# Down projection of an RWKV-7 and MLP kernel: from one plain product to seven half-size products

## The chip, the core and the metric

The kernel runs on one core of a Trainium2 chip. A core has five engines that run side by side, each with its own list of instructions worked off in order: TensorE (PE in the profile, with its weight loads as PEld), VectorE (DVE), ScalarE (ACT), GpSimd (POOL) and SyncE (SP), which here only issues transfers (DMAs). TensorE reads its operands in SBUF and writes its results to PSUM; the others bring them from PSUM to SBUF. The metric is the device time of one execution in microseconds.

## The reference

The reference is an RWKV-7 recurrence whose output goes through a two-layer MLP. Cut to what matters:

```
state = zeros(4, 8, 40, 40)                     # batch, heads, 40 x 40
for t in range(768):
    y[:, :, t] = einsum('bhd,bhde->bhe', r_t, state)
    Sa    = einsum('bhde,bhe->bhd', state, a_t)
    state = state * w_t - einsum('bhd,bhe->bhde', Sa, b_t) + einsum('bhd,bhe->bhde', v_t, k_t)
x = y.transpose(0, 2, 1, 3).reshape(3072, 320)   # 4 * 768 tokens
h = x @ w_in                                     # 320 -> 2048
g = h / (1 + exp(-1.702 * h))
out = g @ w_out                                  # 2048 -> 320
```

The change is about the last line. All arithmetic is float32.

## The kernel before

The 768 steps are cut into 12 chunks of 64 steps. A chunk is worked as two units of two batches each (24 units, `i`; chunk `c`, half `p`). For a unit, the attention part solves the recurrence inside the chunk with small matrix products (PSUM tiles `ps_N`, `ps_level`, `ps_Q`, `ps_T`, `ps_B`, `ps_X`, `ps_y` and so on), each followed by a copy or an elementwise operation on ACT, DVE or POOL, and most of these feed the next product. The unit's output is written to DRAM and read back in another layout into `xT_all`, which has three slots, one for each chunk (`part_with`, `get_back`).

The MLP (`mlp(c)`) works on the 256 tokens of a chunk. `up` makes the hidden layer in four quarters `q` (`ps_up`); `gelu` (L1000) brings each quarter from PSUM into a tile `g` with 512 hidden channels: `g_of(n)` is [128, 2, 2, 256], that is half-quarter `m`, block `f`, 256 tokens, of which 128 belong to each unit `p`. Then `down(p)` makes the output for the 128 tokens of one unit: eight parts `m`, each 2 blocks x 4 array quarters of 64 x 64, with 320 columns moving, all into one PSUM pair (two banks, one for each row half). `finish` brings it out: a copy of one bank (L1027, ACT or DVE), an addition of the other (L1029, DVE), and two stores on SP. Only the very last unit is cut into two column halves of 160. A float32 product takes two passes, so each `mm` (L301) shows as two matmul records, each with its own weight load: 16 records for a part.

The heart of the order is a list written out by hand. `plan.add` collects 2709 tasks in the order in which the program text adds them, with their dependences. The string `ORDER` then lists them as they are issued: the task's number, the engine that takes it (`p` PE, `a` ACT, `d` DVE, `g` POOL, `s` SP), and the PSUM pair (0 to 3) or, for transfers, how many may be under way. The costs given to `plan.add` stand only for whoever made the list; at run time the list alone counts. Each engine works its tasks strictly in that order, so a task that waits holds up all that stands behind it on its engine.

SBUF is nearly full: `w_sb` holds both weight matrices, `extra` is scratch for the conversion of the weights at the start and free afterwards, and `plan.slots` says how many buffers each tile has.

Of the kernel before, what the change touches and what calls it, by code (L numbers as in the profile page):

```python
# [109 lines left out]
0s 8s 1s4 5s 102a 7s 6s 3a 9s 157a 87p0 88p1 10s 89a1 100p2 90a0 95d 13s4 4a 11s 93d 12s 101d2 98p3 2s 94d 97d 17s 103p1 16s 96d  # L110
142p0 15s 104a1 105d1 141p2 143a0 106d 99d3 107p1 144a2 18s4 148g 132p3 108a1 109d1 155p0 45s4 149d 27s 150g 156d0 158p2 14s4
110p1 159a2 160d2 91s4 130p0 161d 19a 24s4 112d1 162p2 111a1 22d 26s4 25s 163a2 113p1 20d 131a0 152g 164d2 34s4 92a 272s 21d
165p0 114a1 151g 271s 147a 153p2 115d1 273s 166a0 167d0 116p1 23g 28a 154d2 262p0 343s 117d1 263p2 133a3 342s 264a2 118d1 168p3
36s 31d 33s 119p1 276g 169a3 170d3 35s 120d1 42s 122a1 171p2 277d 278g 121a 43s 124d1 123a1 126p3 173d2 125a1 127d3 285a 29d
128p1 172a2 44s4 286p3 30d 54s4 37a 174p2 129d1 32g 51s4 288d3 134p1 178a2 146s4 175d2 145s 265a0 135d1 176a 187p0 289d 136p1
275s4 179a2 266g 61s 38d 138d1 188a0 341s 139s 287a3 181p0 39d 185p3 40d 137a1 177a2 290p1 313d 180a2 182a0 53s4 280g 279g 274s
186a3 183p2 292d1 281p0 291a1 333p3 41g 184d2 332p1 282d0 189p2 334a3 60s4 345s 314p0 190d2 316a0 346d 355a 191p3 347d 315d0
193d3 356p2 344s2 62s 140s 194s 195s4 192d3 293p0 335a1 358d2 46a 283p3 359d 317p1 294a0 295d0 349g 318a1 284d3 360p0 269a 348d
350g 296p1 336d 361a0 362d0 319p3 383d 357a2 297a1 298d1 384p0 321p2 49d 320a3 299p1 385a0 47d 322a2 63s4 363p3 300a1 301d1
323d2 386a0 302p1 364a3 365d3 353p0 351p2 306a1 48d 267s3 207p3 52s3 307a1 305d1 208p3 50g 268s3 64a 303d1 209p3 352d2 210p3  # L120
211p3 354d0 308a1 196p2 304a 212p3 65d 197p2 213p3 72s3 214p3 70s3 270d 55a 309p1 337s3 198p2 69s4 366p0 310a1 66d 199p2 367a0
200p2 58d 468p1 201p2 368d0 469a 473s 202p2 476s 203p2 67d 387p0 477s 470a1 490d 204p2 68g 480s 339a 205p2 369p1 388d0 206a2
215p3 371d1 218p0 219p0 56d 472s4 216p3 483g 71s4 220p0 217a3 471d 81s4 221p0 482d 79s 311p2 222p0 370a1 223p0 224p0 312d2 225p0
340d 372p3 229p1 478s4 376a3 230p1 57d 378a3 324p2 560s4 377a3 59g 226p0 78s4 375a3 325d2 231p1 73a 232p1 227p0 373d3 326p2 374d
228a0 389p3 484g 479s3 327d2 338s4 240p0 529d 390a3 481g 328d2 379p3 233p1 380a3 329d 234p1 391p2 485g 241p0 556s4 392d2 80s4
242p0 393d2 74d 486p3 235p1 487d3 530p2 236p1 75d 531a2 381p3 237p1 532a2 330s4 382d3 238p1 76d 491p2 394p3 494a2 493d2 77g
239a1 243p0 395d3 82a 488p1 557s3 396p3 489d1 474a 558s4 83d 331s 251p1 492d2 495d 252p1 84d 85d 253p1 398d3 86g 559s4 548p2
244p0 703s 397d3 549a 570d 553s 245p0 496d 550a2 552s 399d 497a 254p1 551g 554a 498p3 564d 400s 568p2 565g 499a3 246p0 569d2
500d3 563g 247p0 562d 694p2 561g 255p1 248a0 401s2 249d0 475d 256p1 250s 533p3 257p1 534a3 555d 695a 571p0 535p3 573d0 258p1
574a0 698s4 501d 696a2 609d 502g 536a3 537p2 572d0 259a1 576d 566p3 538a2 702s 402p0 575g 567d3 577a 403p0 404p0 539d2 785s3  # L130
700a 405p0 706s 708d 406p0 578p3 407p0 580d3 408p0 260d1 610p2 409p0 581d 709g 410p0 611d2 411p0 612d2 503p1 707d 582g 412a0
424p2 425p2 504d1 704s2 426p2 505d1 427p2 697d 428p2 579d3 613p1 701d 429p2 614a1 583p0 430p2 584a0 506d 431p2 585d0 432p2 507a
782s2 586d 433p2 587d 446p3 434a2 508p1 588p0 509a1 447p3 590d0 589a0 510d1 261s2 413p2 511d 699s 414p2 591d 512a 783s 415p2
592g 416p2 513p0 417p2 514a0 515d0 593p1 516d 418p2 594a1 595d1 419p2 596d 420p2 517a 597d 421p2 422p2 518p0 423a2 435p1 519d0
436p1 521d0 520g 437p1 522d0 438p1 523d0 439p1 440p1 524d0 525p2 716p0 526a2 441p1 717d0 927s 442p1 718d0 527p2 443p1 719d0
444p1 528d2 598p0 721d 445a1 540p2 720d 722g 601d0 603a0 617p1 602d0 541d2 448p3 618a1 604d0 542p2 619d1 599d0 600d 615p1 705s
544d2 449p3 616a1 781s 710d 545g 711d 605p0 723p1 606a0 450p3 607p0 451p3 546s 608d0 930s 452p3 725d1 724d1 620p0 726d 543d2
727a 773p1 453p3 621d0 778s 774a 547s 754d 728p2 622p0 454d3 455d3 729d2 456s 457p3 775a1 776g 730d2 784s 786g 779a 777s 624d0
458p3 623d0 625g 731d 793p1 833d 732a 459p3 733p2 789g 460p3 626s 734a2 794d1 735d2 714p0 790g 736d 461p3 780d 737g 1009s 918p1
755p2 923s 462p3 715d0 756a2 627s 757a2 788d 463p3 738p0 787d 464p3 739a0 740d0 919a 795p2 465d3 758p0 1006s 466d3 798a2 921d  # L140
650p3 467s 759d0 920a1 651p3 924a 928s 796d2 712p1 797d2 652p3 922s 800d 799g 653p3 932d 801a 654p3 834p0 655p3 713d1 656p3
657p3 835d0 760p2 836d0 925d 658p3 761a2 659p3 762p1 660a3 741d 628p0 742d 926s 629p0 630p0 763d1 802p2 764d1 631p0 803a2 804d2
632p0 805d 633p0 806a 743p3 634p0 746d3 635p0 747d3 837p1 931g 748d3 636p0 838a1 1007s 749d3 637p0 807p2 744d3 933g 638a0 639p1
808d2 640p1 791p3 745a 809d2 672p0 810d 792d3 811a 750p2 641p1 751a2 812p3 642p1 813a3 814d3 752p2 643p1 753d2 644p1 815d 645p1
816a 765p3 839p2 766d3 646p1 840a2 647p1 817p3 648p1 818a3 819d3 767p2 820d 649a1 821d 673p0 769d2 929s 768d2 770g 822p3 934d
674p0 825a3 826a3 940p1 827a3 675p0 1151s 828a3 935d 943a1 771s 661p2 823d3 662p2 941d1 1154s 824a 663p2 942d1 997p3 945d 944g
664p2 998a 1002s 978d 938p1 946g 665p2 939d1 666p2 772s 667p2 668p2 829p1 669p2 999a3 1000d 1001s 830d1 670p2 1003a 1011d 676p0
671a2 1004d 831p3 841p1 677p0 832d3 1005s 842d1 936p3 843d1 678p0 937d3 844p2 679p0 845d2 947p1 1010g 680d0 846p3 948a1 681d0
1012d 682s 683p2 847d3 1013g 1008s 848d3 1019p0 1014g 949d1 684p2 1022a0 1230s 849d 1233s 979p3 685p2 980a3 950d 850s 1020d0
981a3 951g 1142p1 1021d0 686p2 1024d 1143a 1147s 1023d 1025g 982p3 1057d 687p2 1152s 952p0 851s 983a3 1145g 688p2 1156d 1146s  # L150
953a0 954d0 984p3 1144a1 955d 1148a 689p2 956d 985a3 1149d 986p0 690p2 987a0 1150s 988d0 957p1 691a2 863p3 958a1 692d2 864p3
959d1 865p3 693s 960d 866p3 961d 1026p0 867p3 1027a0 1028d0 868p3 1029d 1155g 869p3 1157d 1030a 1058p2 870p3 871p3 1059a2 872p3
1060d2 1031p1 873a3 852p0 1033d1 853p0 1034d 854p0 1035d 1061p2 855p0 1062d2 1032a1 856p0 962p3 857p0 963a3 964d3 1036p1 965d
858p0 1037a1 1038d1 859p0 1039d 1015p2 966a 1040g 860p0 1016d2 861p0 967p3 862a0 874p1 968d3 875p1 970d3 969g 1041p2 971d3 876p1
1042a2 972d3 877p1 973d3 878p1 879p1 1043d2 1017p0 1044d 974p3 1045a 880p1 1018d0 1231s 881p1 975a3 1164p2 882p1 1167a2 1165d2
1375s 976p0 883p1 1166d2 896p3 1169d 1168g 884a1 977d0 885p2 1170a 1046p0 989p1 1049a0 886p2 1050a0 990d1 887p2 1051a0 888p2
1052a0 889p2 1047d0 991p1 1048a 1065p0 992d1 1158g 1153s 890p2 1159d 1066a0 891p2 892p2 1067d0 1378s 893p2 1202d 1063p0 993d1
894p2 994d 1064a0 1229s 1053p1 897p3 895a2 1054d1 995s 1171p0 1221p2 898p3 1172a0 1173d0 1226s 1174d 1222a 1175g 1055p1 899p3
1056d1 1068p0 996s 1162p1 1223a2 1224d 1234g 1225s 1069d0 900p3 1227a 1163d1 1160p2 901p3 1236d 1161d2 902p3 1235d 1176p0 1228d
903p3 1177a0 1178d0 1243p1 904a3 1179d 1070p2 1246a1 1454s 905d3 1180g 1244d1 906s 1245d1 907p0 1248d 1232s 1237g 1071d2 1249a  # L160
908p0 1238g 1072d2 1247d 1181p3 1457s 1281d 1366p1 909p0 1182a3 1073d 1371s 910p0 1183d3 1367a 1074s 1184d 1250p2 1185d 911p0
1368a1 1369g 1370s 1380d 1251a2 1186p3 1252d2 1372a 912p0 1253d 1188d3 1254g 1075s 1187a3 1189d 1241p1 1373d 913p0 1190g 1255p2
# [87 lines left out]
def rwkv7_gelu_quick(ctx: ExitStack, tc: tile.TileContext, time_d, v_d, w_d, wc_d, ak_d, b_d, rv_d, w_in, w_out, out):  # L250
# [13 lines left out]
    EARLY = 4  # L264
    BY_PE = 4
    PLAIN = 4
    PARTS = 4
    ROUNDS, WINDOW, SHARE = 4, 5000.0, 1.0
    RANKS = [14, 16, 20, 24, 35, 37, 39, 41]
    HALF = [slice(0, 64), slice(64, 128)]  # L270
# [716 lines left out]
    def mlp(c):  # L987
# [16 lines left out]
        def down(p):  # L1004
# [28 lines left out]
            for n, cols in enumerate([slice(0, DM // 2), slice(DM // 2, DM)] if last else [slice(0, DM)]):  # L1033
                for m in range(NM):
                    part(m, n, cols)
# [7 lines left out]
        for p in BITS:  # L1043
            down(p)
# [105 lines left out]
```

## Time and profile before

| what | before |
|---|---|
| runs | 677.32, 679.32 and 683.4 us (median 679.32) |
| profiled execution, first to last instruction | 677.7 us |
| PE busy, weight loads busy | 649.6 us (96%), 568.7 us (84%) |
| DVE, ACT, POOL busy | 449.7 us (66%), 329.1 us (49%), 175.7 us (26%) |
| down product (`ps_down`), matmul records | 3200 |
| up product (`ps_up`), matmul records | 3840 |
| bytes moved | 69.74 MB |

The execution in the profile has a span of 677.7 us; no other time is given for it, and it lies 0.4 us above the lowest of the three runs and 1.6 us below their median. Each row of a group of instructions reads: line, engine, operation, out<-in, partitions x elements, count | busy time, mean duration in ns | idle time of the engine just before them, and what ended it. Matmul records overlap each other, because a matmul's own duration includes its way through the array; the spacing of many records in a row, as the chain of waits gives it (start, length, how many), says more than a mean.

### The profile page before, as it was taken

To read this page: it belongs to the slowest core of one execution; us is meant where nothing else is said; L and a number is where in the kernel's file an instruction comes from. 1 tells how busy PE (TensorE), PEld (TensorE's weight loads), DVE (VectorE), ACT (ScalarE), POOL (GpSimd) and SP (SyncE) were. 2 spreads that over 40 slices of the span, in tenths; PEclk is the share of its full clock that TensorE was granted. 3 is DMA by queue.
4 is the path that set the end of the run, shared out by engine and by line. 5 is a ranking of instruction groups with operands and counts; after the bars stand their busy time and mean duration, and the time that the engine had idled before them with its cause. 6 is when DMAs were issued, how large, how long until landed. Compare 5 with 4: busy or idle time off the path is not lost.

```text
span 677.7 us, 42447 instructions
## 1 busy us (share of the span) xinstructions
PE 649.6 (96%) x19616; PEld 568.7 (84%) x19616; DVE 449.7 (66%) x916; ACT 329.1 (49%) x681; POOL 175.7 (26%) x201
## 2 busy tenths in 40 slices
PE   5777999999999999999999999999999999999997
PEld 4667787787999997888888899999889798799896
DVE  5777779777867668757776687868656766675001
ACT  3676745634564655654545445455344454263010
POOL 6541443324123123123113211322411421300000
PEclk9979999999999999999999999999999999999999
DMA  6875753415324314432404513513412411200200
GB/s 208 295 255 160 226 172 97 129 42 152 107 64 131 94 58 124 114 107 65 124 14 131 149 35 108 155 33 107 140 38 62 130 53 45 69 15 14 60 13 21
DMA packets 35473, 69.74 MB, mean 103 GB/s; under 512 B 5472, under 2 KB 14816, under 8 KB 35296
## 3 DMA queue, kind: packets, MB, share of 16 engines
q1 hardware_dynamic: 35216, 66.99, 32.9%
q8 instruction: 154, 2.52, 1.6%
q14 instruction: 23, 0.19, 0.1%
q10 hardware_dynamic: 80, 0.04, 0.0%
HBM read 59.15 MB, written 7.86 MB: 99 GB/s over the span
## 4 chain that ended last, share of the span: by engine, by line
PE 88%; DMA 6%; DVE 2%; issue 1%; SPq 1%; ACT 1%; DVEq 0%; ACTq 0%
PE ps_up L301 31%; PE ps_down L301 29%; PE ps_level L301 8%; PE ps_y L301 5%; PE ps_B L301 4%; PE ps_X L301 2%; PE ps_N L301 2%; PE ps_rz L301 1%; PE ps_RV L301 1%; PE ps_A L301 1%; PE ps_zT L301 1%; SPq L331 1%; DMA w_sb<-in_w_in 1%; PE ps_cum L301 1%; PE ps_T L301 1%
## 5 line engine op out<-in xcount | busy, mean ns | idle before, releaser
L301 PE MATMUL ps_up<-xT_all,w_sb 64*64 64x256 f32 x3840 | 253.3, 377 | 2.1 <-issue 1.3
L301 PE MATMUL ps_down<-w_sb,g 64*64 64x320 f32 (+1 forms) x3200 | 241.5, 419 | 0.2 <-ACT zr L879 0.2
L301 PEld LDWEIGHTS ps_up<-xT_all,w_sb 64*64 64x64 f32 x3840 | 170.8, 133 | 18.8 <-issue 2.1
L301 PEld LDWEIGHTS ps_down<-w_sb,g 64*64 64x64 f32 x3200 | 142.5, 133 | 31.6 <-issue 0.4
L1000 ACT ACTIVATE g<-ps_up 128x1024 f32<-128x1024 f32 x48 | 49.2, 1025 | 46.3 <-PE ps_up L301 45.8
L719 POOL TENSOR_TENSOR EX<-ES,quads 128x512 f32<-128x512 f32 x30 | 39.7, 1324 | 116.4 <-DVE ES L712 77.7
L761 ACT COPY W<-ps_level 128x512 f32<-128x512 f32 x56 | 32.8, 585 | 67.7 <-PE ps_level L301 66.0
L301 PEld LDWEIGHTS ps_level<-W,EX 64*64 64x64 f32 x2560 | 60.0, 134 | 5.4 <-DVE T L840 0.2
L763 DVE TENSOR_TENSOR E<-two,ps_level 128x256 f32<-128x256 f32 x80 | 33.1, 415 | 36.5 <-ACT W L761 32.3
L301 PE MATMUL ps_level<-W,EX 64*64 64x64 f32 (+1 forms) x2560 | 56.8, 217 | 0.0
L717 ACT ACTIVATE EX<-ES,quads 128x256 f32<-128x256 f32 x82 | 37.2, 501 | 31.9 <-DVE ES L712 31.3
L629 POOL TENSOR_TENSOR ak<-ak,FT 128x512 f32<-128x512 f32 x17 | 23.0, 1353 | 77.2 <-DMA ak<-in_ak 54.4
L301 PEld LDWEIGHTS ps_level<-PT,EX 64*64 64x64 f32 x1280 | 30.7, 138 | 11.5 <-DVE EX L733 3.3
L301 PE MATMUL ps_level<-PT,EX 64*64 64x64 f32 (+2 forms) x1280 | 32.5, 234 | 6.9 <-DVE EX L733 5.0
L712 DVE STREAM_TRANSPOSE ES<-E 128x256 f32<-128x256 f32 x80 | 35.3, 443 | 4.4
L301 PE MATMUL ps_y<-RV,kh 64*64 64x104 f32 (+1 forms) x768 | 35.4, 247 | 0.9 <-DVE M L917 0.9
L301 PE MATMUL ps_y<-M,bh 64*64 64x104 f32 (+1 forms) x768 | 35.5, 247 | 0.7 <-DVE M L917 0.5
L901 ACT COPY B<-ps_B 128x416 f32<-128x416 f32 (+1 forms) x35 | 17.2, 493 | 34.4 <-PE ps_B L301 34.2
L301 PEld LDWEIGHTS ps_y<-RV,kh 64*64 64x64 f32 x768 | 29.6, 133 | 3.2 <-DVE M L917 1.5
L917 DVE TENSOR_TENSOR M<-ps_X,later 128x832 f32<-128x832 f32 (+1 forms) x24 | 23.9, 995 | 10.2 <-PE ps_X L301 10.0
L301 PE MATMUL ps_B<-RV,A 64*64 64x104 f32 (+1 forms) x768 | 29.2, 252 | 0.8 <-issue 0.8
L637 POOL TENSOR_TENSOR kh<-time,G 128x320 f32<-128x320 f32 x18 | 16.2, 901 | 51.2 <-PE ps_y L301 34.6
(133 smaller groups left out, 1099.0 us busy)
## 6 DMA issues: line engine op xcount, KB each, us to landing
ak<-in_ak SPq DMA_DIRECT2D x48, 160.0 KB
rv<-in_rv SPq DMA_DIRECT2D x48, 160.0 KB
time<-in_time SPq DMA_DIRECT2D x24, 320.0 KB
xT_all<-x_dram SPq DMA_DIRECT2D x48, 160.0 KB
wc<-in_wc SPq DMA_DIRECT2D x20, 264.0 KB
logw<-in_w SPq DMA_DIRECT2D x24, 160.0 KB
RV<-in_v SPq DMA_DIRECT2D x24, 160.0 KB
b<-in_b SPq DMA_DIRECT2D x48, 80.0 KB
```

The costliest lines, as they stand in the source:

```text
L301: nc.tensor.matmul(o, lhsT, rhs, start=start, stop=True, skip_group_check=True)
L331: begun.append(queue.dma_start(dst, src).ins)
L629: plan.add(R, {"DVE": 690.0, "POOL": 1270.0, "sbuf": True}, lambda t: of(t.engine).tensor_mul(ahT(), ahT(), FT_of(i)), reads=T("ak", "FT") ...
L637: plan.add(R + 4, {"POOL": 870.0, "DVE": 490.0, "sbuf": True}, lambda t, n=n, dst=dst: of(t.engine).tensor_mul(dst(i)[:, :, :D], by_head(t ...
L712: plan.add(rank, dve(256), lambda t: nc.vector.transpose(ES(n), source(t)), writes=[key("ES", n, 6)], **reads)
L717: nc.scalar.activation(dst[:, :, h], ES(n), ACT.Copy, scale=quads[:, h, :1])
L719: of(t.engine).tensor_mul(dst, ES(n).unsqueeze(2).to_broadcast([128, 8, 2, 32]), quads.unsqueeze(1).to_broadcast([128, 8, 2, 32]))
L761: plan.add(rank, any2(512), lambda t: copy(t.engine)(tiles_of(W(n + 1)), blocks(psum(t, ""), 64)), writes=[key("W", n + 1, 5)], pair=pair)
L763: plan.add(rank, dve(256), lambda t: nc.vector.tensor_sub(tiles_of(E(n + 1)), every(two32, [128, 2, 4, 32]), blocks(psum(t, ""), 64)[:, :, ...
L901: plan.add(R, any2(4 * wide), lambda t: copy(t.engine)(dst(), some(psum(t, "")[:, :, :208])), writes=[("Bv", i)] if x and c > 0 else T("B" ...
L917: plan.add(R + 1, dve(8 * wide), lambda t: nc.vector.tensor_tensor(M_of(i)[:, :, :wide].rearrange("p (j b) n -> p b j n", b=2), some(psum( ...
L1000: plan.add(-45, {"ACT": 1030.0, "table": "gelu"}, lambda t: nc.scalar.activation(g_of(c * NQ + q).rearrange("p m r n -> p r m n"), psum(t, ...
```

## The change

For chunks 1 to 11 (`FAST = 1`; chunk 0 keeps the plain product, now `plain`) the down product of a chunk is seen as a product of 2 x 2 blocks: A (256 tokens x 2048 channels) in token halves `p` and channel halves `m`, and B (`w_out`) in channel halves `m` and column halves of 160 (`HD`). Instead of eight block products, seven are made, by Strassen's scheme in Winograd's form:

- Sums of blocks of A, 128 x 256 elements for each quarter `q`: S1 = A22 - A21, S3 = A21 - A11 (in place of A21), S2 = S1 + A11, and S4 = A12 - S2 (in place of A12, once product 2 has read it). They are 16 tensor_tensor instructions a chunk, each on DVE or POOL as `ORDER` says: 67 of the 176 on DVE and 109 on POOL.
- Sums of blocks of B, made once (`weight_sums`): four instructions of 128 x 1280, three on DVE and one on POOL, into `extra`.
- Seven products (`times`), each of four parts of 16 matmul records, 64 x 64 weights and 160 columns. Products 1, 2 and 4 collect in the PSUM pair `fa`, 6, 5 and 7 in `fb`, 3 in `fc`.
- Bringing them out: for `fa` and `fb` a copy and a DVE addition of 480 columns each; five additions in SBUF on DVE or POOL (`cd`, `E`, `F`, `Q` and the output of token half 1); two DVE additions of 160 columns from `fc`; then two store tasks.

Places: S1 takes the third slot of `xT_all`, which leaves two for x; S2 overwrites the B12 block of `w_out` in SBUF, which is not read after the sums of B and chunk 0's product; the results of all products of a chunk lie in one buffer `sb` with a single slot, in place of `ob`. To make room, `wz` is now kept in place in `wch`, and two constants share a tile. The last unit is no longer cut in two.

`ORDER` has 3087 tasks. Up to the first part of chunk 0's down product the two lists name the same tasks on the same engines; behind it the order is new, and many other tasks have another engine: of the 24 x 4 block copies into `Tc`, DVE has 35 tasks instead of 52; of the outputs `x` (L962), 21 instead of 13; of the `W` copies (L761), 34 instead of 24; of the `zT` copies, 10 instead of 20; of the `P` copies (L702), 11 instead of 2.

```
-                     ... x=1, xT=3, g=4, ob=1), 4)
+                     ... x=1, xT=2, g=4, sb=1, S1=4, S2=4), 4)
...
-    wz_of = lambda i: buf("wz", i, [128, 8])
+    wz_of = lambda i: wch_of(i)[:, 0]
...
+    block = lambda n, p, m: g_of(n)[:, m, :, p * 128:p * 128 + 128]
+    S1_of = lambda n: xT_all[:, 2, (n % NQ) * 256:(n % NQ) * 256 + 256].rearrange("p (f t) -> p f t", f=2)
+    w_blocks = w_out_sb.rearrange("p (q m f n) -> p q m f n", q=NQ, m=2, f=2)
+    B = lambda m, n: w_blocks[:, :, m, :, n * HD:(n + 1) * HD]
+    S2_of = lambda n: w_blocks[:, n % NQ, 0, :, HD:HD + 128]
+    sums = extra.rearrange("p (k q f n) -> p k q f n", k=4, q=NQ, f=2)
+    def weight_sums():
+        made = [(0, B(0, 0), B(0, 1), ALU.subtract, []), (1, B(1, 1), sums[:, 0], ALU.subtract, [("sum", 0)]),
+                (2, B(1, 1), B(0, 1), ALU.add, []), (3, B(1, 0), sums[:, 1], ALU.subtract, [("sum", 1)])]
...
+        def fast():
...
+                combined(q, "S1", S1_of, a22, a21, ALU.subtract, [("weight", raws.index("x"))], [("S1", n)])
+                combined(q, "S3", a21, a21, a11, ALU.subtract, [("S1", n)], [("S3", n)])
+                combined(q, "S2", S2_of, S1_of, a11, ALU.add, [("S1", n), ("sum", 0), ("sum", 2)] + none, [("S2", n)])
+            def times(name, q, group, slot, left, right, reads, writes=[], first=False):
...
+                    for f in BITS:
+                        for r, b in QUARTERS:
+                            mm(ps[HALF[b], r, slot * HD:(slot + 1) * HD], a[HALF[r], f, b * 64:b * 64 + 64], right[HALF[r], q, f],
+                               fresh and f == 0)
...
+                times("1", q, "fa", 0, lambda n: block(n, 0, 0), B(0, 0), lambda n: [("g", n), ("weight", NQ + q)])
+                times("2", q, "fa", 1, lambda n: block(n, 0, 1), B(1, 0), ... , lambda n: [("P2", n)])
+                times("4", q, "fa", 2, lambda n: block(n, 1, 1), sums[:, 3], lambda n: [("g", n), ("sum", 3)])
+                combined(q, "S4", a12, a12, S2_of, ALU.subtract, [("S2", n), ("P2", n)], [("S4", n)])
+            evicted("fa", 0, 0)
+            add(lambda: sb_of(c)[:, 4::2], twice(0), sb(1, 2), wide, [("fa", c)], [("cd", c)])
+                times("6", q, "fb", 0, S2_of, sums[:, 1], lambda n: [("S2", n), ("sum", 1)])
+                times("5", q, "fb", 1, S1_of, sums[:, 0], lambda n: [("S1", n), ("sum", 0)])
+                times("7", q, "fb", 2, lambda n: block(n, 1, 0), sums[:, 2], lambda n: [("S3", n), ("sum", 2)])
+            evicted("fb", 1, 0)
+            add(sb(7), sb(0), sb(2), two, [("fb", c), ("fa", c)], [("E", c)])
+            add(sb(5), sb(7), sb(1), two, [("E", c), ("fb", c)], [("F", c)])
+            add(sb(3), sb(3), sb(1), two, [("fb", c)], [("Q", c)])
+            add(sb(6, 2), sb(6, 2), twice(3), wide, ... , [("out", 2 * c + 1), ("sb", c)])
+                times("3", q, "fc", 0, lambda n: block(n, 0, 1), B(1, 1), lambda n: [("S4", n), ("weight", NQ + q)])
+            for r in BITS:
+                plan.add(-45, dve(HD), lambda t, r=r: nc.vector.tensor_add(sb(5)(), sb(5)(), psum(t, "")[:, r, :HD].unsqueeze(1)), ...
```

The end of the new list, from the last hidden quarters of chunk 11 on, has on PE the parts of product 1, then 2 and 4 with those of 6 put between them, then 5, 7 and 3; on DVE, behind the addition of `fb`, stand `E`, `Q`, `F`, the output of token half 1, and then the two additions from `fc`.

More of the change, by code (lines that the diff above doesn't have):

```diff
@@ L114 @@
[L114 to L117, printed above, removed]
@@ L1013, in go @@
                             o = p * 128 + b * 64
-                            mm(po[HALF[b], r, :cols.stop - cols.start], g[HALF[r], f % 2, o:o + 64],
-                               w_out_sb[HALF[r], f * DM + cols.start:f * DM + cols.stop], f == 0)
+                            mm(po[HALF[b], r, :DM], g[HALF[r], f % 2, o:o + 64], w_out_sb[HALF[r], f * DM:(f + 1) * DM], f == 0)
                 parts = range(2 * m * DM // PIECE, (2 * (m + 1) * DM - 1) // PIECE + 1)
-                plan.add(R + 10 * (p + 1) + m + 8 * n, pe((2, cols.stop - cols.start)), go, reads=[("g", c * NQ + m // 2)] + [("weight", NQ + n) for n in parts],
-                         pair=("down", serial + n), most=1)
@@ L1020, in finish @@
-            def finish(n, cols):
-                ob, wide = lambda: ob_of(serial)[:, cols], cols.stop - cols.start
-                def store(t):
-                    for b in BITS:
-                        o = (2 * p + b) * S + c * C
-                        transfer(t, out[o:o + C, cols], ob()[HALF[b]], nc.scalar if last and n and b else nc.sync)
-                plan.add(-45, any2(wide), lambda t: copy(t.engine)(ob(), psum(t, "")[:, 0, :wide]),
-                         writes=[("ob", serial + n)], pair=("down", serial + n))
-                plan.add(-45, dve(wide), lambda t: nc.vector.tensor_add(ob(), ob(), psum(t, "")[:, 1, :wide]),
-                         reads=[("ob", serial + n)], writes=[("out", serial + n)], pair=("down", serial + n))
-                plan.add(-100, {"SP": 700.0}, store, reads=[("ob", serial + n), ("out", serial + n)], size=128 * wide * 4)
@@ L1033, in down @@
-            for n, cols in enumerate([slice(0, DM // 2), slice(DM // 2, DM)] if last else [slice(0, DM)]):
-                for m in range(NM):
-                    part(m, n, cols)
-                finish(n, cols)
+                plan.add(R + 10 * (p + 1) + m, pe((2, DM)), go, reads=[("g", c * NQ + m // 2)] + [("weight", NQ + n) for n in parts],
+                         pair=("down", serial), most=1)
+            for m in range(NM):
+                part(m)
+            ob = lambda: sb_of(c)[:, 4 + 2 * p:6 + 2 * p].rearrange("p h n -> p (h n)")
@@ new lines, in plain @@
+            plan.add(-45, any2(DM), lambda t: copy(t.engine)(ob(), psum(t, "")[:, 0, :DM]),
+                     writes=[("ob", serial)], room=[("sb", c)], pair=("down", serial))
+            plan.add(-45, dve(DM), lambda t: nc.vector.tensor_add(ob(), ob(), psum(t, "")[:, 1, :DM]),
+                     reads=[("ob", serial)], writes=[("out", serial), ("sb", c)], pair=("down", serial))
+            plan.add(-100, {"SP": 700.0}, lambda t: store(t, c, p), reads=[("out", serial)], uses=[("sb", c)], size=128 * DM * 4)
@@ L1042, in mlp @@
             gelu(q)
-        for p in BITS:
-            down(p)
+        if c < FAST:
+            for p in BITS:
+                plain(p)
+        else:
+            fast()
     for i in range(3):
@@ L1052, in rwkv7_gelu_quick @@
     weights()
+    weight_sums()
     for i in range(NU):
```

370 lines of the change are left out of this document (225 added, 145 removed).

## The prediction

> **What bounds the kernel now.** I read the page first, then the busy time by stage, then what PE waits for. From the page:
>
> ```profile
> span 677.7 us, 42447 instructions
> PE 649.6 (96%) x19616; PEld 568.7 (84%) x19616; DVE 449.7 (66%) x916; ACT 329.1 (49%) x681; POOL 175.7 (26%) x201
> ...
> PEclk9979999999999999999999999999999999999999
> ...
> PE 88%; DMA 6%; DVE 2%; issue 1%; SPq 1%; ACT 1%; DVEq 0%; ACTq 0%
> ```
>
> PE is busy 96% of the span, at the full granted clock but for the start, and holds 88% of the chain that ended last. A busy PE need not be the bound, so the stages, with busy time and instructions of each engine:
>
> ```profile
> core 0: us, PE busy (x) PEld busy (x) DVE busy (x) ACT busy (x) POOL busy (x), PEclk, DMA share, GB/s
> 0.00:100.00 100.00, 77.99 (x2598) 66.48 (x2600) 72.76 (x123) 59.64 (x141) 44.52 (x62) 0.97 0.69 219
> 100.00:600.00 500.00, 497.82 (x15286) 435.71 (x15279) 355.82 (x738) 252.33 (x515) 131.21 (x140) 1.00 0.32 92
> 600.00:678.00 78.00, 73.80 (x1755) 66.55 (x1746) 21.11 (x57) 17.10 (x27) 0.00 (x0) 0.99 0.09 24
> ```
>
> In the 500 us from 100 on PE lacks 2.2 us; in the first 100 it lacks 22. So behind the opening the kernel is a stream of matmuls, and what shortens it shortens the kernel, as long as nothing makes PE wait. The first 100 us hardly change: the two lists part at chunk 0's first down part, which this profile has at about 88 us.
>
> **What the stream gains.** The forms of the down product, and two stretches of the chain (start, length, records) in which it runs alone:
>
> ```profile
> L301 PE MATMUL ps_down<-w_sb,g 64*64 64x320 f32 x2944 | 232.8, 430 | 0.2 <-ACT zr L879 0.2
> L301 PEld LDWEIGHTS ps_down<-w_sb,g 64*64 64x64 f32 x3200 | 142.5, 133 | 31.6 <-issue 0.4 <-ACT zr L879 0.4
> L301 PE MATMUL ps_down<-w_sb,g 64*64 64x160 f32 x256 | 8.9, 296 | 0.0
> ```
>
> ```profile
> 626.30 10.77 PE ps_down L301 x159
> 659.72 14.10 PE ps_down L301 x336
> ```
>
> The stretch at 626 is ten parts of 320 columns (160 records, one missing): 10.77 / 10 = 1.077 us a part. The one at 659 is five such parts (80 records) and the 256 records of 160 columns: 14.10 - 5 x 1.077 = 8.71 us, or 34.0 ns a record and 0.544 us for a part of 16. That is the very form of the new products (64 x 64 weights, 160 columns), and it costs half of 1.077 and 6 ns more: halving the columns and doubling the weight loads is nearly free. A chunk has 16 wide parts now, 16 x 1.077 = 17.23 us, and will have 7 x 4 = 28 narrow ones, 28 x 0.544 = 15.24. That is 1.99 us less in ten chunks; the last, now 8 x 1.077 + 8.71 = 17.33, gives 2.09. Together **-22.0 us**. Chunk 0 keeps its product.
>
> Here a rule of the skill speaks against the change. The records of 133 ns for a weight load beside a set of four narrow matmuls in 4 x 34.0 = 136 ns leave little cover. The Trainium skill ("TensorE: Matmul & The Clock Gate", section "Back-to-back issue gap") says that pairs of weight load and matmul are spaced by both, 81 ns at 128 columns where the matmul alone takes 56: 25 ns more. Charged to each of 112 sets in 11 chunks this estimate is +31 us, and the term would be +9 instead of -22. The 256 narrow records measured here show no such 25 ns.
>
> **What the other engines get.** Rows for the new work (instructions of like size; in the second group the columns are count, then min/median/max in ns):
>
> ```profile
> L1027 ACT COPY ob<-ps_down 128x320 f32<-128x320 f32 x15 | 6.4, 426 | 29.6 <-PE ps_down L301 28.5 <-DMA xT_all<-x_dram 0.6 <-DMA rv<-in_rv 0.5
> L879 ACT COPY zr<-ps_rz 128x512 f32<-128x512 f32 x12 | 7.0, 586 | 21.0 <-PE ps_rz L301 20.9
> L1029 DVE TENSOR_TENSOR ob<-ob,ps_down 128x320 f32<-128x320 f32 x23 | 11.1, 482 | 19.8 <-ACT ob L1027 19.5
> L660 DVE TENSOR_TENSOR RV<-ps_RV,upper 128x512 f32<-128x512 f32 x24 | 16.2, 679 | 8.5 <-PE ps_RV L301 8.4
> L1029 DVE TENSOR_TENSOR ob<-ob,ps_down 128x160 f32<-128x160 f32 x2 | 0.6, 321 | 3.7 <-ACT ob L1027 3.7
> ```
>
> ```profile
> L707 DVE TENSOR_TENSOR PT<-two,PT x10: 381/416/1220, 102.9 to 536.2; 128x256 f32<-128x256 f32 x10
> L707 POOL TENSOR_TENSOR PT<-two,PT x10: 725/730/734, 119.9 to 591.3; 128x256 f32<-128x256 f32 x10
> L855 DVE TENSOR_TENSOR zr<-zraw,wz x22: 443/482/1562, 46.0 to 583.7; 128x320 f32<-128x320 f32 x22
> L962 DVE TENSOR_TENSOR x<-zr,FT x52: 275/280/1365, 89.8 to 627.7; 128x128 f32<-128x128 f32 x52
> L719 POOL TENSOR_TENSOR EX<-ES,quads x30: 1272/1280/1685, 118.6 to 597.7; 128x512 f32<-128x512 f32 x30
> ```
>
> DVE: 67 sums of 128 x 256 at 0.416 (L707) are 27.9 us. 22 additions of 480 columns from PSUM lie between 0.482 and 0.679, I take 0.64: 14.1. Four copies of that size on DVE, 2.6. 24 of the small additions at 0.31 to 0.48 (L962 to L855), 9. 22 additions of 160 columns at 0.321, 7.1. Three sums of weights, 1280 wide: by the step from 256 (0.416) to 512 columns some 1.5 us each, 4.5; the fourth, on POOL, some 3. PE needs the sums only from product 4 of chunk 1 on, and by the list 12 us of its other work lie between. Gone are 23 wide and two narrow `ob` additions but two, and all but one of DVE's `ob` copies, -14.5. The tasks that changed engine cancel to about +2 on DVE (fewer `Tc`, `zT` and spread tasks, more `W`, `x` and `P` ones). That is +53 us. POOL: 109 sums at 0.730 are 80 us, 31 small additions some 19, less 8 of moved work: +94 with the weight sum, to about 270. ACT gains about 9 and stays near half. All this is beside PE, and costs nothing while it is in time.
>
> What it does to DVE is the open price. Some 49 of the 53 us fall in the middle, which shrinks from 500 to about 479: 355.8 + 49 = 405 us, 85% instead of 71%. And the rows show DVE held up by POOL: with two inputs from SBUF the median of L855 is 482 ns, but the longest took 1562, 1.08 us more, most of a POOL instruction of L719. The mean excess of such DVE instructions is 0.08 us in L962 (mean 362, below), 0.15 in L707 (568), while the same operation with an input from PSUM has none (276):
>
> ```profile
> L962 DVE TENSOR_TENSOR x<-zr,FT 128x128 f32<-128x128 f32 x52 | 15.8, 362 | 0.2
> L962 DVE TENSOR_TENSOR x<-ps_y,FT 128x128 f32<-128x128 f32 x8 | 1.7, 276 | 0.5 <-PE ps_y L301 0.5
> L707 DVE TENSOR_TENSOR PT<-two,PT 128x256 f32<-128x256 f32 x10 | 5.7, 568 | 0.0
> ```
>
> POOL's share in the middle goes from 26% to about 46%, and some 340 DVE instructions with two SBUF inputs stand where some 230 did. At 0.07 us on the average now and, with POOL's share, 0.125 then, that is some 25 us more, and DVE is near 90%. Its list is worked in order, so work that comes late reaches PE. What PE waits for now, longest first:
>
> ```profile
> PE ps_level L301 <- DVE EX L733: 5.0, 6, 1.0
> ...
> PE ps_up L301 <- DMA xT_all<-x_dram: 0.6, 1, 0.6
> PE ps_zT L301 <- DVE zr L855: 0.6, 1, 0.6
> ```
>
> L733 belongs to the first four units, whose levels have a form of their own. For the middle I let the 2.2 us grow as DVE's free share shrinks, from 29 to 10%: 6.4, so **+4**. No row shows this directly. From below it is -2 (the new order removes today's waits), from above +12: each of the 11 chunks then loses about 1.1 us, one POOL sum of 0.73 and half of another, on some tight edge. I take the value near the lower end, since the list leaves the sums room: in most chunks the parts of 1, 2 and 4 (12 x 0.544 = 6.5 us) stand between the last `gelu` and product 6, and the chain `gelu`, S1, S2 is 1.02 (L1000 on the page) + 2 x 0.73 = 2.5. S4 has products 6, 5 and 7 for cover, another 6.5 us. Without that cover a chunk would pay up to 2.5 us.
>
> **Moved steps, queues and waits.** With two slots for x, the return of chunk c waits for `up` of chunk c-2, done a whole chunk before (some 45 us); free. The way through DRAM is 4.06 + 3.94 us and PE waits 0.6 for it in the whole run; uncovered it would cost 8 once. The single `sb` lets the copy out of `fa` wait for the stores of the chunk before; some 30 us of PE work lie between the last product of one chunk and the end of `fa` in the next, and a store lands in about 3. SP issues 24 stores instead of 25. PE gets 2 x 1984 more instructions (5184 down records instead of 3200), 10% of its list; its waits for issue are 1% of the chain, so 0 to 1 us, inside the +4.
>
> **The end.** There nothing hides the last steps. Now:
>
> ```profile
> 673.84 0.32 DVE L1027 COPY ob<-ps_down 128x160 f32<-128x160 f32 x1 [3.70 <-PE ps_down L301]
> 674.20 0.32 DVE L1029 TENSOR_TENSOR ob<-ob,ps_down 128x160 f32<-128x160 f32 x1
> 674.55 0.47 SPq L331 DMA_DIRECT2D out<-ob  x1
> 674.55 0.55 ACTq L331 DMA_DIRECT2D out<-ob  x1
> ```
>
> The last store is issued about 0.8 us after PE's end (673.8) and the span ends 3.15 later. Then: product 7 ends four parts, 2.18 us, before PE's end; behind it come the wait for PE (0.15), the ACT copy of 480 columns (0.426 to 0.586, say 0.55), the DVE addition 0.64, `E`, `Q`, `F` at 0.31, the output at 0.48 and the two additions of 0.321, with 0.04 between them: 3.7. So the issue comes 1.5 us after PE's end instead of 0.8, and SP has two other stores in front, 2 x 0.47, partly beside the rest: **+1.2** (0.7 to 2).
>
> **The sum.** 677.7 - 22.0 + 1.2 + 4 = 660.9 us for an execution like the profiled one. The median of the runs lies 1.6 above it and the lowest 0.4 below, so I add 1: **662**. A measurement of this kernel tells about 1% from no change.
>
> **The rivals.** *DVE becomes the bound.* If the blocking by POOL is not 0.125 but 0.25 us an instruction, DVE has 405 + 58 us plus some 850 gaps of 0.04 between instructions (674.16 to 674.20 above), 497 us where 479 are to be had: 18 us longer, which take the place of the +4, so 657 + 18 = 675 (667 to 679). For it speaks that the longest records lose nearly a whole POOL instruction; against it that half of them start while POOL idles. The Trainium skill ("SBUF — State Buffer", section "Who interferes with whom") states this blocking as lasting for the other's whole instruction; the maxima agree, the medians show how seldom it is met.
>
> *The weight loads show.* A set of narrow matmuls then takes 17.23 / 112 = 154 ns instead of 136 and the gain is nil: 678 to 681, within 1%. The 256 records at 34.0 ns speak against it, but they are one stretch, with little other traffic.
>
> *PE waits at the sums (slower).* PE takes its list in order; product 6, 5, 7 or 3 in front of it waits for a sum, and the attention products behind it wait too. It decides from 20.8 / 11 = 1.9 us a chunk on, which is two and a half POOL sums late. With the whole chain S1, S2, S4 and the `gelu` uncovered, 3.2 us a chunk, it gives 677.7 - 20.8 + 35 = 692. The 6.5 us of cover in the list speak against it; for it, that spreads of 1.28 us (L719) stand between the sums on POOL.
>
> **How the numbers follow.** The forecast (PE stays the bound, 655 to 669) gets 0.72, DVE as the bound 0.14, the weight loads 0.06, PE waiting at the sums 0.08. The range of 654 to 676 holds nearly all of the first and half of the second, and leaves out about 2 in 10. Faster by over 1% (below 672.5): 0.72 + 0.06 + 0.02 = 0.80; within 1%: 0.08 of the second, 0.04 of the third, 0.12; slower by over 1%: 0.08.
>
> **What would show it.** In the profile after: `ps_fast` of 64 x 160 with 4928 records at 34 ns each in a stretch, else the first term is wrong; PE's lack between 100 and 600 us below 10 us; DVE near 90% there and no more; L855, L962 and the sums with longer means than now; no wait of PE for POOL over a few us in total; the last issue 1.5 us behind PE. If PE's waits name POOL or DVE for over 20 us, the forecast is wrong.

## The result, and the profile after

The changed kernel takes 724.02 us (median of 4 runs, 721.33 to 728.09), the kernel before 679.37 (4 runs, 677.32 to 683.4): a ratio of 1.0645, interval 1.0596 to 1.0694. The forecast was 662, so it is off by 62 us, and on the other side. The profiled execution took 724.27 us, with a span of 722.3.

From the page of after, and below it one line of the page of before that the prediction did not look at (queue, kind: packets, MB, share of 16 engines' time):

```profile
span 722.3 us, 46673 instructions
...
PE 655.3 (91%) x21600; PEld 603.3 (84%) x21600; DVE 502.1 (70%) x1024; ACT 338.3 (47%) x716; POOL 271.8 (38%) x317
...
q8 instruction: 170, 2.79, 1.6%
...
PE 80%; DVE 7%; issue 7%; DMA 2%; ACT 2%; POOL 1%; SPq 0%; DVEq 0%; ACTq 0%; POOLq 0%
```

```profile
q8 instruction: 154, 2.52, 1.6%
```

DVE's busy time grew by 52 us and POOL's by 96, and neither is near full (the forecast was 94 for POOL, and for DVE 53 of work and some 25 of blocking). Yet PE is idle: its share fell from 96 to 91%, and in the chain that ended last "issue" (PE waits, and nothing that the profile follows releases it) rose from 1% to 7%. By stage:

```profile
0.00:100.00 100.00, 79.25 (x2507) 73.10 (x2508) 71.31 (x121) 58.59 (x138) 42.24 (x61) 0.93 0.69 216
100.00:600.00 500.00, 463.64 (x15581) 429.35 (x15584) 367.52 (x762) 245.32 (x508) 195.62 (x214) 0.99 0.29 87
600.00:722.30 122.30, 112.39 (x3520) 100.89 (x3512) 63.23 (x143) 34.36 (x70) 33.96 (x43) 0.99 0.14 39
```

Between 100 and 600 us PE lacks 36 us (2.2 before), while DVE is at 74% and POOL at 39%. What PE waits for (total us, times, longest), after:

```profile
PE ps_fast L323 <- issue: 8.5, 14, 1.2
PE ps_level L323 <- issue: 8.2, 8, 2.4
PE ps_RV L323 <- issue: 5.3, 5, 2.2
PE ps_cum L323 <- POOL logw L400: 3.8, 1, 3.8
PE ps_level L323 <- DVE EX L756: 3.3, 4, 1.0
PE ps_N L323 <- issue: 3.2, 3, 1.6
PE ps_level L323 <- POOL ak L657: 3.0, 1, 3.0
```

The long rows name no engine and no transfer; the waits for engines in this list belong to the first units or happen once. Waits for "issue" in front of four kinds of products, which read different things, speak against a cause in what they read. The timeline shows its rhythm (start, us, line, tiles, records, idle before):

```profile
402.08 0.51 PE L323 MATMUL ps_RV<-rv 40*64 40x64 f32 x19 [0.70 <-issue]
...
402.48 2.34 PE L323 MATMUL ps_fast<-extra,xT_all 64*64 64x160 f32 x62
...
409.55 0.63 PE L323 MATMUL ps_N<-b,ak 40*64 40x64 f32 x28 [0.27 <-issue]
...
413.85 1.18 PE L323 MATMUL ps_fast<-w_sb,g 64*64 64x160 f32 x27 [1.17 <-issue]
```

The trace's packets of queue q8 and the records between two stalls of PE fit together. In this stretch (worked out from the single records):

```
q8 packet lands at     396.54   400.54   404.30   408.06   412.37
PE resumes at          398.13   402.08   405.55   409.55   413.85
later by                 1.59     1.54     1.25     1.49     1.48
matmul records since              127      128      127      128
```

A matmul record goes with one weight load (x21600 and x21600 in the page), so 127 or 128 records are 256 instructions, and 2.79 MB / 170 is 16.4 KB a packet, 64 bytes for each of them. The count agrees: 43,200 instructions / 256 = 168.8 for 170 packets, and before 39,232 / 256 = 153.3 for 154. So q8 brings PE's own list of instructions, and here PE stands at the end of each packet until some 1.5 us after the next has landed. The packets start 3.2 us apart at the least and 3.9 in the median.

Counted over all records behind 100 us: gaps in PE's work beyond what the records' columns explain (over 40 ns each, some 70 ns of ordinary spacing taken off) are 4.0 us in before, 2.2 of them ending 1.15 to 1.65 us behind a packet; in after they are 54.0 us, 42.3 of them (65 gaps) behind a packet. By chance that window would hold 12% of them. What is taken off moves these totals by some us and the comparison not. Below, "gaps behind a packet" and "others" are counted in the same way, each from one trace.

Cut into blocks of 128 records, before has 13 of 132 blocks behind 100 us whose columns (0.211 ns each, by the 33.5 to 34.0 ns of a record of 160) are worth less than 3.3 us, and after has 66 of 148. Those 66 took 3.6 us each on the average, 47 us more than their columns, of 83 us in all blocks; in before the 13 took 3.5 us more, of 20. That is the pattern; whether it is the cause is for the experiments.

**Theory F**, the instruction packets: PE is fed 256 instructions per 3.3 to 3.9 us at best. Where 256 instructions stream in less time, the packets set the pace, and halving the columns of a matmul halves nothing. **Rival S**: PE waits for the sums S1 to S4, made on DVE and POOL. **Rival W**: the new order itself has waits, whatever stands in it. The expectations also name a **theory N**: narrow matmuls show the time of their weight loads.

### The profile page after: what moved, and what is told of

Its sections match the earlier page's. It is cut to its first block, busy times and chain, and to the rows that moved or that the text cites. A ratio compares the mean times of both kernels' runs of the same rounds, so it can differ in the third digit from the quotient of the medians.

```text
span 722.3 us, 46673 instructions
## 1 busy us (share of the span) xinstructions
PE 655.3 (91%) x21600; PEld 603.3 (84%) x21600; DVE 502.1 (70%) x1024; ACT 338.3 (47%) x716; POOL 271.8 (38%) x317
## 3 DMA queue, kind: packets, MB, share of 16 engines
q8 instruction: 170, 2.79, 1.6%
## 4 chain that ended last, share of the span: by engine, by line
PE 80%; DVE 7%; issue 7%; DMA 2%; ACT 2%; POOL 1%; SPq 0%; DVEq 0%; ACTq 0%; POOLq 0%
PE ps_up L323 27%; PE ps_fast L323 22%; PE ps_level L323 9%; PE ps_B L323 4%; PE ps_y L323 4%; PE ps_X L323 2%; DVE x L985 2%; PE ps_down L323 2%; PE ps_N L323 2%; PE ps_A L323 2%; PE ps_rz L323 1%; PE ps_RV L323 1%; PE ps_zT L323 1%; PE ps_cum L323 1%; PE ps_Q L323 1%
## 5 line engine op out<-in xcount | busy, mean ns | idle before, releaser
L323 PE MATMUL ps_fast<-w_sb,g 64*64 64x160 f32 x2112 | 94.4, 300 | 2.7 <-issue 2.7
L323 PEld LDWEIGHTS ps_fast<-w_sb,g 64*64 64x64 f32 x2112 | 76.9, 134 | 4.8 <-issue 4.0
L1043 ACT ACTIVATE g<-ps_up 128x1024 f32<-128x1024 f32 x48 | 49.0, 1024 | 56.7 <-PE ps_up L323 54.5
L740 ACT ACTIVATE EX<-ES,quads 128x256 f32<-128x256 f32 x102 | 46.0, 502 | 52.0 <-DVE ES L735 52.0
L323 PE MATMUL ps_fast<-extra,g 64*64 64x160 f32 x1408 | 61.3, 297 | 3.2 <-issue 2.9
L323 PEld LDWEIGHTS ps_fast<-extra,g 64*64 64x64 f32 x1408 | 51.3, 133 | 5.0 <-issue 4.9
L784 ACT COPY W<-ps_level 128x512 f32<-128x512 f32 x46 | 26.9, 585 | 60.9 <-DVE E L786 40.0
L1108 POOL TENSOR_TENSOR sb<-sb 128x160 f32<-128x160 f32 (+1 forms) x31 | 21.2, 690 | 70.6 <-DVE sb L1103 53.2
L1077 POOL TENSOR_TENSOR xT_all<-g 128x256 f32<-128x256 f32 x29 | 22.3, 773 | 65.9 <-ACT g L1043 65.9
L830 ACT COPY Tc<-ps_level 32x64 f32<-32x64 f32 x122 | 24.7, 203 | 31.8 <-DVE ES L735 11.5
L985 DVE TENSOR_TENSOR x<-zr,FT 128x128 f32<-128x128 f32 x84 | 37.3, 504 | 0.4
L735 DVE STREAM_TRANSPOSE ES<-E 128x256 f32<-128x256 f32 x80 | 34.2, 434 | 2.9 <-DVE E L786 0.5
```

Source lines behind the costliest of these rows:

```text
L323: nc.tensor.matmul(o, lhsT, rhs, start=start, stop=True, skip_group_check=True)
L735: plan.add(rank, dve(256), lambda t: nc.vector.transpose(ES(n), source(t)), writes=[key("ES", n, 6)], **reads)
L740: nc.scalar.activation(dst[:, :, h], ES(n), ACT.Copy, scale=quads[:, h, :1])
L784: plan.add(rank, any2(512), lambda t: copy(t.engine)(tiles_of(W(n + 1)), blocks(psum(t, ""), 64)), writes=[key("W", n + 1, 5)], pair=pair)
L830: copy(t.engine)(dst, src[:, u, :, f])
L985: of(t.engine).tensor_mul(x[:, b ^ u, b], y, FT_of(i)[:, at])
```

## The experiments

**The parts of a product with half the instructions.** In the changed kernel, `times` makes each part from 8 records of 320 columns instead of 16 of 160; sums, order and stream stay.

```
-                    for f in BITS:
-                        for r, b in QUARTERS:
-                            mm(ps[HALF[b], r, slot * HD:(slot + 1) * HD], a[HALF[r], f, ...], right[HALF[r], q, f], fresh and f == 0)
+                    at = min(slot, 1) * HD
+                    for r, b in QUARTERS:
+                        mm(ps[HALF[b], r, at:at + 2 * HD] ..., a[HALF[r], 0, ...], right[HALF[r], q], fresh)
```

> The changed kernel, but each part of a product is made of 8 matmul records of 320 columns instead of 16 of 160: the same array time (0.539 us a part instead of 0.544), half the instructions, and the sums are made and waited for as before. It leaves out half of each product (one block f of the left side), so the output is not the reference's. Theory F (PE's instructions arrive in packets of 256 and no faster than one in about 3.4 us): PE has about 4900 fewer instructions, fewer than before the change, and its waits for issue nearly vanish; 655 to 670 us. Theory S (PE waits late sums and a busy VectorE, and the profile fails to name them): nothing changes, 715 to 725 us. Theory N (narrow matmuls show their weight loads in traffic): also faster, about 690 us, but then the gaps of the changed kernel would lie anywhere and not one packet apart.

Measured: 689.68 us, ratio to before 1.0113 (1.0020 to 1.0207), 150 packets. Some 34 of the 45 us that the change cost are gone although the sums and the order are as they were, which S has no place for. But it is not the 655 to 670 of F either; the time is that of the third case, N, whose other sign fails, since the gaps of the changed kernel do lie one packet apart in the stretch above, and the larger part of them behind a packet. Gaps behind a packet fell to 10.1 us, others are 17.0 (11.7 in after). So the instructions of the parts carry the larger share of the loss and not all of it. What about them it is, the next runs separate: in the second only instructions are added, in the old order, and in the one behind the last product narrow records run by themselves.

**Nothing but more instructions.** The kernel before, its order, engines and stream untouched; three of four down parts of chunks 1 to 11 are issued as two halves of 160 columns (cut to the lines that matter).

```
+                        wide = cols.stop - cols.start
+                        step = 160 if c > 0 and m % 4 != 3 else wide
+                        for at in range(0, wide, step):
                             for r, b in QUARTERS:
-                                mm(po[HALF[b], r, :cols.stop - cols.start], ...)
+                                mm(po[HALF[b], r, at:at + step], ...)
```

> The kernel before, with three of four down parts of chunks 1 to 11 cut into two column halves of 160: 5216 down records, as many as the changed kernel has (5184), with no sums, no new order and nothing else. The array time grows by 126 x 0.011 = 1.4 us. Theory F: the gaps of the changed kernel appear here too, 705 to 730 us. Theory S: 680 to 683 us. Theory N: like F by time, so the place of the gaps must tell.

Measured: 728.26 us, ratio 1.0679 (1.0569 to 1.0789), 170 packets. What its PE waits for, from its trace:

```profile
PE ps_down L301 <- issue: 8.1, 13, 1.3
PE ps_level L301 <- issue: 6.8, 9, 2.0
PE ps_cum L301 <- POOL logw L377: 3.8, 1, 3.8
PE ps_level L301 <- DVE EX L733: 3.3, 4, 1.0
PE ps_RV L301 <- issue: 3.2, 3, 1.5
```

No sum, no new order, no Strassen product, and the loss is as large as that of the whole change, with the same signature: 35.2 us of gaps behind a packet and 3 of others. So 33 of the 47 us are gaps behind a packet, and what the rest is stays open. This is the clearest of the runs.

**Fewer parts split.** As above with `m % 2 == 0` (every second part, two thirds of the added instructions).

> The same with every second part cut: 4608 down records, array time +1.0 us. Theory F: between the kernel before and the run with three of four, 690 to 708 us. Theory S: 680 to 683 us.

Measured: 706.18 us, ratio 1.0355 (1.0253 to 1.0458), 165 packets; the trace has 4544 down records, not the 4608 expected. The gaps behind a packet are 19.3 us, against 2.2 with no part split and 35.2 with three of four. The time rises with the count of instructions: 25 us for two thirds of the added ones, 47 for all.

**The changed kernel without its sums.** The 16 sums of each of the chunks 2 to 11 are not issued.

```
-  ... lambda t: of(t.engine).tensor_tensor(out=out(n), in0=x(n), in1=y(n), op=op),
+  ... lambda t: of(t.engine).tensor_tensor(out=out(n), in0=x(n), in1=y(n), op=op) if c == FAST else None,
```

> The changed kernel with the sums of blocks of A left out in chunks 2 to 11 (160 instructions on VectorE and GpSimd; the products read what stands there, so the output is not the reference's). VectorE and GpSimd lose some 25 and 73 us and no product waits for a sum. Theory F: PE's instructions are the same, 710 to 722 us. Theory S: the loss goes, 660 to 672 us.

Measured: 727.94 us, ratio 1.0674 (1.0577 to 1.0771), even a little above F's range. Rival S falls as what bounds this kernel: with the sums away nothing is gained. In the two traces the gaps behind a packet are 53.0 us instead of 42.3, the others about 6 instead of 11.7.

**Both at once**: half the instructions of the parts and no sums.

> Both at once: the changed kernel with products of half the instructions (8 records of 320 columns a part, half of each product left out) and without the sums of chunks 2 to 11 (the output is not the reference's). Behind 100 us the run with half the instructions still had some 10 us of gaps that end about 1.4 us after a packet of instructions has landed, and 17 us of others. Theory F with late sums as the second part: the others shrink to about 5, the first stay; 672 to 680 us. If the sums cost nothing beside the fetch: 686 to 690 us, as with them.

Measured: 679.17 us, ratio 0.9971 (0.9927 to 1.0016). Against the first run the ratio is lower by 0.0142, give or take 0.0104, about 10 us (3 to 17): so the sums do cost time once the packets bind less, and none that can be told while they bind: the packets hide what the sums cost. The time came as expected, the gaps did not: 5.9 us behind a packet and 13.3 of others, where about 10 and 5 were expected.

**The limit by itself.** The kernel before with five runs of 512 products (1024 records, 2048 instructions, 8 packets each) behind its last product, all with operands that lie in SBUF, of 64 to 256 columns.

```
+    for wide in (64, 96, 128, 160, 256):
+        ps = banks.tile([128, 2, 512], FP32, tag="pair0", name=f"ps_run{wide}")
+        for n in range(128):
+            for r, h in QUARTERS:
+                mm(ps[HALF[h], r, :wide], w_sb[HALF[r], 64 * n:64 * n + 64], w_sb[HALF[r], 64 * n:64 * n + wide], True)
```

> The kernel before, and behind it five runs of matmuls that nothing waits for and that wait for nothing: 512 each of 64, 96, 128, 160 and 256 columns, 2048 instructions or eight packets each. By columns alone they take 15.9, 21.2, 28.1, 34.9 and 55.4 us. Theory F: no run takes less than eight packets times 3.3 to 3.9 us, so the first three take 27 to 31 us each, with a gap at every packet, and the last two their own time. Theories S and N: every run goes by its columns; for N with a fixed cost of the weight loads, so also the 160 run is longer than 35.

Measured in one execution (855.47 us), the beginning of the 64-column run from its timeline:

```profile
682.13 2.10 PE L301 MATMUL ps_run<-w_sb 64*64 64x64 f32 x128 [1.65 <-issue]
685.88 2.10 PE L301 MATMUL ps_run<-w_sb 64*64 64x64 f32 x128 [1.65 <-issue]
689.35 2.10 PE L301 MATMUL ps_run<-w_sb 64*64 64x64 f32 x128 [1.38 <-issue]
```

PE works 128 records, stands still, and goes on 1.2 to 1.5 us after the next packet has landed, seven times in a row. All five runs, from the groups of the trace (busy us, mean ns | idle before, and for what):

```profile
L301 PE MATMUL ps_run<-w_sb 64*64 64x256 f32 x1024 | 55.5, 376 | 0.1
L301 PE MATMUL ps_run<-w_sb 64*64 64x160 f32 x1024 | 35.0, 296 | 0.1
L301 PE MATMUL ps_run<-w_sb 64*64 64x128 f32 x1024 | 29.5, 270 | 0.7 <-issue 0.6
L301 PE MATMUL ps_run<-w_sb 64*64 64x96 f32 x1024 | 23.3, 244 | 7.1 <-issue 7.0
L301 PE MATMUL ps_run<-w_sb 64*64 64x64 f32 x1024 | 16.8, 219 | 10.0 <-issue 10.0
```

Busy and idle together: 55.6, 35.1, 30.2, 30.4 and 26.8 us. Down to 160 columns the time follows the columns. The 128-column run takes 2 us more than its columns (28.1), with short gaps at five of its packets; 96 columns take no less than 128, and 64 columns take 3.35 us for 256 instructions where their own work is 2.1. With nothing else on the core but the last stores, this leaves no other engine, sum or order to blame, and N's weight loads would not put the time at every 128th record. A pure run of 160 columns, at 35.1 / 8 = 4.4 us a packet, is still free of it: the 34.0 ns of the prediction were right, and could not show the limit. In the chunks these records alternate with attention products of 64 columns, which spend 256 instructions in 2.1 us, and then the mixture falls below 3.3 to 3.9: the 66 blocks counted above are of this kind. Before, 320 columns took 8.6 us for 256 instructions (128 x 1.077 / 16) and made up for them.

**One place of the new order mended.** At 111 us PE waits longest behind the opening. In after, from VectorE's, GpSimd's, ScalarE's and TensorE's timelines:

```profile
108.05 5.28 DVE L985 TENSOR_TENSOR x<-zr,FT 128x128 f32<-128x128 f32 x4
113.26 0.43 DVE L735 STREAM_TRANSPOSE ES<-PT 128x256 f32<-128x256 f32 x1
```

```profile
107.21 2.96 POOL L496 TENSOR_TENSOR w_sb<-w_sb,extra 128x1280 int32<-128x1280 int32 x1 [2.35 <-DVE w_sb L488]
110.12 0.92 POOL L660 TENSOR_TENSOR bh<-time,G 128x320 f32<-128x320 f32 x1
111.01 0.92 POOL L660 TENSOR_TENSOR kh<-time,G 128x320 f32<-128x320 f32 x1
111.88 1.31 POOL L652 TENSOR_TENSOR ak<-ak,FT 128x512 f32<-128x512 f32 x1
```

```profile
113.73 0.91 ACT L740 ACTIVATE EX<-ES,quads 128x256 f32<-128x256 f32 x2 [5.99 <-DVE ES L735]
```

```profile
114.73 0.69 PE L323 MATMUL ps_level<-PT,EX 64*64 64x64 f32 x32 [3.00 <-POOL ak L657]
```

The row names POOL's `ak`, which ended at 114.46, but the product reads `PT` and `EX`. What PE needs is the transpose `ES` (L735) and the `EX` that ScalarE makes from it until 114.64, and the transpose stands behind four small steps that take 5.28 us where four of 0.28 would be 1.1. The test puts this task behind the transpose:

```
-... 402d2 401d2 403d 535d 534g ...
+... 402d2 401d2 535d 403d 534g ...
```

> The changed kernel (724.0 us) with one task moved: VectorE's four steps of unit 3 on x (L985), which stand ahead of the ES transpose at 108 us, go right behind it. In the trace of after PE idles 3.2 us there, behind that transpose, and has half its clock for 3.4 us after it. If this order is what costs the time (theory W: the new order's own waits), place by place, this one place gives 3.2 us of idle time and some 1.7 us of half clock back: 719, between 717 and 721. If the instruction packets bind behind it (theory F), a place like this is partly paid back, since packets come on while PE waits: 722 to 726, no change that three rounds can tell.

Measured: 724.79 us, ratio 1.0640 (1.0587 to 1.0693): no change that can be told from the 1.0645 without the move, as F expects. It is weak evidence against W: the difference of the two ratios is known to some 5 us, which is what W expects to gain, and the upper end of W's 717 to 721 stays possible. The repair itself worked: PE reaches this product at 111.26 us, while POOL still works on `ak` until 114.58, and from 105 to 120 us it is busy for 13.49 us instead of 12.00, at the full granted clock instead of 0.89 of it. Over the whole kernel the gaps not behind a packet fell from 11.7 to 8.0 us, and those behind a packet rose from 42.3 to 46.0. These are single traces, and the one with the move is 3.2 us shorter (719.1 against 722.3), in a kernel whose executions spread over 7 us. So it is not shown whether the packets took back what was gained at the place.

**The same move where the packets bind less**, in the kernel with halved parts and without sums.

> The same move in the kernel with halved parts and without sums (679.2 us), where the packets hardly bind. Both theories: the place's 3.2 us and the half clock behind it come back, if that kernel shows the same stall, 674 to 677; no change, 678 to 680, if PE finds the same wait elsewhere.

Measured: 678.21 us, ratio 0.9977 (0.9946 to 1.0007), the same as without the move (0.9971) to within some 4 us. The kernel without the move does show the stall (4.08 us, ending at 116.30), so 674 to 677 were due; the time missed them, by too little to be certain. The gaps moved in the traces: others from 13.3 to 7.9 us, behind a packet from 5.9 to 11.7. So even this kernel is close to the limit, and the runs can't say what the order costs by itself.

No run beats the kernel before by an amount that can be told. The first run shows how far off that is: even with wide parts and half their instructions it is at 1.0113, and without the sums too at 0.9971, although the stream is then worth some 20 us less than before. Beside it 38 us are lost behind 100 us, against 20 before, and more of their gaps lie away from the packets than behind them. So a part of the loss is not the packets' and points at the new order; its cause stays open.

## Why the prediction was wrong, step by step

- **What bounds the kernel** ("a stream of matmuls, and what shortens it shortens the kernel"): right for before, where PE waited for almost nothing, but PE's list was close to a second limit that costs nothing until it is crossed: 677.7 / 154 = 4.4 us a packet on the average.
- **The first term, -22.0**: right as far as it goes. `ps_fast` has 4928 records; 62 of them in the stretch at 402.48 last 2.34 us, of which 0.30 are the last one's own record: 2.04 us for 61 turns, 33.5 ns. Valued by their columns, the records behind 100 us are worth 554 us before and 533 after, 21 less. From 100 us to the start of the last matmul it took 573.5 before and 616.9 after, so what lies beside the stream grew from 20 to 84 us, by 64.
- **The step that failed** is the last one of "Moved steps, queues and waits": "PE gets 2 x 1984 more instructions [...], 10% of its list; its waits for issue are 1% of the chain, so 0 to 1 us, inside the +4". The 40 us more of gaps behind a packet are that step. An average of before was taken for a price per instruction, where the runs show a threshold: 256 instructions in less than some 3.3 to 3.9 us make PE wait, and in the runs by themselves 4.4 us for 256 cost nothing. Splitting the down products of before and nothing else cost 47 us (728.26 against 681.24 beside it).
- **The waits, +4**: too small, and the basis failed too. DVE did not go to 90%: it was at 74% between 100 and 600 us, where PE had become slower, and its 429 us of busy time from 100 us to the last matmul would be 78% even of the 552 that the forecast left. The forecast added the durations of DVE's records, which grew by 70 us of the 78 it expected; but the records overlap, and the busy time grew by 52. The +4 stood for waits for engines; the gaps not behind a packet grew by some 10 us (1.8 to 11.7), and with half the instructions of the parts by 15 (to 17.0), more than the 12 of the upper bound. The last 14 of the 64 us lie in stalls too short, or in stretches of half clock, to be put down to one cause; these stay open.
- **Blocking by POOL**: right in size on the average. The price was to be 0.125 us for each of some 340 DVE instructions with two SBUF inputs. There are 346 of them, and their mean lies 0.118 us above the medians of their groups (0.082 over 233 before). Most of what was added is in `x`, with 0.22, as the rows show; the others have 0.085. The rival's 0.25 over all does not come out:

```profile
L985 DVE TENSOR_TENSOR x<-zr,FT 128x128 f32<-128x128 f32 x84 | 37.3, 504 | 0.4
L985 DVE TENSOR_TENSOR x<-ps_y,FT 128x128 f32<-128x128 f32 x8 | 1.8, 284 | 0.5 <-PE ps_y L323 0.5
```

- **The end, +1.2**: right. From the start of the last matmul to the end of the span it is 5.4 us (716.9 to 722.3) after, and 4.2 (673.5 to 677.7) before.
- **The rivals.** *DVE becomes the bound*: no, by its share. *The weight loads show*: no, by the 33.5 ns. *PE waits at the sums* (692) gave the right sign, but not for its reason: without the sums the time is the same. The cause was none of the three, and the range of 654 to 676 held no place for it. Of the marks that were to show it wrong, PE's lack (36 us instead of below 10) did so, while POOL and DVE were not named.

The Trainium skill ("Runtime: NRT & Kernel Launch", section "Instruction fetch mechanics") describes the blocks: an engine's instructions come in 16 KiB pieces of 256, and the next piece is brought while the present one is worked. The packets here agree (16.4 KB, 127 or 128 pairs). It also says that crossing a block is "mostly hidden". In before that holds (2.2 us in 6 gaps); in the changed kernel it does not (42.3 us in 65 gaps).

## What to carry to other kernels

Count PE's instructions as well as its columns: matmuls and weight loads together, 256 a packet, and beside each stage the time in which its packets would be worked: where that comes near 3.3 to 3.9 us, a scheme that saves arithmetic by narrower matmuls may save no time. Waits for "issue" that recur every 127 or 128 records were the mark of this limit here, and a small share of them before the change said nothing of how near it was. While it held, removing other work or mending a single wait gave nothing back that could be told, so it is the first thing to test, by splitting matmuls in the old kernel.

## What the runs showed of the hardware

- PE's instructions arrive in packets of 16.4 KB no faster than one per 3.2 us; 8 packets in a row took 26.8 us (64 columns) to 30.4 us (96 columns), and PE resumed some 1.5 us after a packet had landed. In the 64-column run three parts make up the interval of 3.5 to 3.8 us: a packet started 1.1 to 1.4 us after PE had resumed, was under way for 0.9 to 1.2 us, and PE went on 1.2 to 1.5 us after it had landed. Why these parts vary was not tried.
- A stall of 3.0 us cost more than itself: behind the one at 111 us the granted clock was half for 3.4 us (116.2 to 119.6), and with the stall mended it was full there. The one at 296 us, 2.2 us of waiting for "issue", had the same behind it (297.1 to 300.5); in the run without sums a stall of the same length there did not.
- Four DVE steps of 0.28 us each took 5.28 us beside POOL instructions of 2.96, 0.92, 0.92 and 1.31 us; each ended some 0.14 us after one of these. Both engines read two inputs from SBUF there.
